# Attention and two MLPs on one core: VectorE's additions moved ahead of its gate ends in MLP 2, early splits taken apart, PSUM accumulators of one bank

## The chip, the cores and the metric

The kernel runs on one core of a Trainium2 chip. The metric is the time of one execution on the device in microseconds (us). All outputs and intermediate results are fp32.

## The reference

The input goes through a chunked attention with memory keys and then through two MLPs. Only MLP 2 is touched by the change:

```
def _moe2_ref(x, w_in, w_out):
    h = x @ w_in                                   # 3072 x 512 @ 512 x 2048
    beta = 1.0
    g = np.where(h >= beta, h, np.where(h <= -beta, 0.0, (h + beta) ** 2 / (4.0 * beta)))
    return (g @ w_out).astype(np.float32)          # 3072 x 2048 @ 2048 x 512

attn_out = _attn_ref(**attn_kwargs)                # softmax(q k) v over 32-token chunks, 8 memory keys
x = attn_out.transpose(0, 2, 1, 3).reshape(B * S, H * D)
x = _moe_ref(x=x, **moe_kwargs)                    # g = h - tanh(h)
return _moe2_ref(x=x, **moe2_kwargs)
```

The gate is the same as max(h, min(relu(h/2 + 1/2)^2, 1)).

## The kernel before

**Arithmetic.** Every fp32 operand of a large matrix product is split into a high part, rounded by ScalarE, and a low part, source minus high part, made by VectorE (`split_to`, L219 to L221). A product of two tiles is then three matmuls: high by high, low by high, high by low. All matmuls of the MLPs have 128 x 128 weights and 512 columns.

**Stages.** Attention and MLP 1 run interleaved over six blocks of 512 tokens (L471 and L506 are MLP 1's two matmuls). From about 574 us on MLP 2 runs, in three blocks (`sb` 0 to 2) of two times 512 tokens. It uses a 2 x 2 scheme of seven block products in place of eight, for both of its matrix products.

**Rounds.** In the first half of a block there are eight rounds `q`. A round has seven products `i` of six matmuls each (`product`), which leave four gates 11, 12, 21 and 22. Three PSUM banks serve a round. Bank a (`qa`, two buffers, from `ps_h`) takes the products 1, 6, 7 and 4, one accumulated on the other; bank b (`qb`) takes 2; bank c (`qc`) takes 5 and 3. Between accumulations ScalarE copies out what was there: u1 after product 1, u2 after 6, v after 5 (L632). The next product on that bank must wait for the copy. The plan's order is: product 1 of round q, then 3 and 4 of round q - 1, then 6, 2, 5 and 7 of round q. In block 0 MLP 1's last 17 output steps stand between.

**Gates.** `gate2` makes a gate in four operations: VectorE adds PSUM and a copy (L642), ScalarE takes relu (L646) and square (L647), and VectorE's *end* takes minimum and maximum (L650). Gate 21 needs no addition and is read from bank a by its relu and by its end. The end is not issued at once: it goes to a list `later`, and `flush` issues the oldest entry behind a later product. Before the change `flush` stood ahead of the gate:

```
name = f"{sb}_{q}"
if i in (3, 6, 2, 7):
    flush()
if i == 1:
    ps[sb, q, "u1"] = take_copy(f"u1_{name}", o)
```

After certain products sums of gates are made (`g_sums`: s1 and s2 at L660 and L661, 21 replaced by a difference at L663).

**Passes.** In the second half of a block seven passes of eight products each go over the rounds' results (`last_product`, L766). Each product takes a split gate or sum (`ghi`, `glo`) as moving operand and adds to two PSUM banks. `prepare` splits; five pairs of slots let it run up to four products ahead, and a table `AHEAD_OF_PASSES` has the first splits made in the late rounds, right behind product 1 (or 5). `done` takes a finished pass out of PSUM. The first passes also carry the sums and splits of the next block's input, on VectorE and ScalarE.

**Order.** The order on each engine is written by hand: an engine works in the order in which the code issues, and waits for what the next instruction needs. SyncE issues all transfers. Temporary 128 x 512 tiles come from a first-in, first-out list of free slots (`take`, `give`); weights stream ten products ahead through the same slots (`load_w`).

Of the kernel before, what the change touches and what calls it, by code (L numbers as in the profile page):

```python
# [8 lines left out]
F32 = mybir.dt.float32  # L9
# [4 lines left out]
AF = mybir.ActivationFunctionType  # L14
ALU = mybir.AluOpType
# [58 lines left out]
def tile_memory_attention_two_mlps(  # L74
# [15 lines left out]
    xsp = ctx.enter_context(tc.tile_pool(name="xsp", bufs=1))  # L90
    dram = ctx.enter_context(tc.tile_pool(name="dram", bufs=1, space=bass.MemoryType.DRAM))
    att = ctx.enter_context(tc.tile_pool(name="att", bufs=2))
    ps_acc = ctx.enter_context(tc.tile_pool(name="ps_acc", bufs=1, space=PSUM))
    ps_h = ctx.enter_context(tc.tile_pool(name="ps_h", bufs=2, space=PSUM))
    pairs = tc.tile_pool(name="ps_a", bufs=1, space=PSUM)
    ps_a = pairs.__enter__()

# [427 lines left out]
        return tag, slot(tag, name, dtype)  # L525

    def give(tag):
        spare.append(tag)

    xc, held, xtags = {}, {}, []  # L530
    XHOME = {1: "xh0", 2: "xl0", 4: "xh1", 3: "xl1", 5: ("k0", "k1"), 6: ("v0", "v1")}
# [136 lines left out]
    bank = {}  # L668

    once = set()  # L670

    def give_second(tag, *key):
        if key in once:
            give(tag)
        once.add(key)

    AHEAD_OF_PASSES = ((6, 1), (6, 5), (7, 1)), ((4, 1), (5, 1), (6, 1), (7, 1))

    def product(e):
        _, sb, q, i = e  # L680
        if i == 1:
            ps[sb, q, "a"] = ps_h.tile([128, 512], F32, tag="h", name=f"qa{sb}_{q}")
        if i == 2:
            ps[sb, q, "b"] = ps_b.tile([128, 512], F32, tag="b", name=f"qb{sb}_{q}")
        if i == 5:
            ps[sb, q, "c"] = ps_b.tile([128, 512], F32, tag="c", name=f"qc{sb}_{q}")
# [12 lines left out]
        if i in (3, 6, 2, 7):  # L699
            flush()  # L700
        if i == 1:
            ps[sb, q, "u1"] = take_copy(f"u1_{name}", o)
        elif i == 6:
            ps[sb, q, "u2"] = take_copy(f"u2_{name}", o)
        elif i == 5:
            ps[sb, q, "v"] = take_copy(f"v_{name}", o)
        elif i == 2:
            gate2(sb, q, "11", o, ps.pop((sb, q, "u1")))
        elif i == 7:
            gate2(sb, q, "22", o, ps.pop((sb, q, "v")))  # L710
        elif i == 3:
            gate2(sb, q, "12", o, ps.pop((sb, q, "u2")))
        else:
            gate2(sb, q, "21", o)
        if 0 < q < HALF - 1 and i == 5:
            g_sums(sb, q - 1, 0)
        if q > 1 and i == 1:
            g_sums(sb, q - 2, 1)
        ahead = AHEAD_OF_PASSES[sb > 0]
        if (q, i) in ahead:  # L720
            prepare(sb, ahead.index((q, i)))
        if sb == 0 and q == 0 and i in (2, 7):
# [5 lines left out]
    def prepare(sb, k):  # L728
        if k >= NG2 or (sb, k) in gsplit:
            return  # L730
        i, q = PASSES[k // HALF], k % HALF
        tag, g = gs[sb, SOURCE[i], q]
        r = prepared[0] % GSETS
        prepared[0] += 1
        hi, lo = slot(f"ghi{r}", f"ghi2_{sb}_{k}", F32R), slot(f"glo{r}", f"glo2_{sb}_{k}", F32R)
        split_to(g, hi, lo)
        if i == 6:
            a12 = gs[sb, "12", q][1]
            nc.vector.tensor_tensor(out=a12, in0=a12, in1=g, op=ALU.subtract)  # L739
# [10 lines left out]
    def last_product(e):  # L750
# [71 lines left out]
    def older(s):  # L822
        output(s)
        fc = steps[s][2]
        if s >= NS - FC:
            give(f"g{fc}")
        if s + 2 < NS:
            split_g(s + 2)
        if s == NS - 1:
            for i in range(W1O):  # L830
                give(f"whi1_{i}")
                give(f"wlo1_{i}")
            for i in range(KC):
# [230 lines left out]
```

## Time and profile before

| | |
|---|---|
| median of 3 runs | 1102.3 us (1102.05 to 1102.45) |
| the profiled execution's own time | 1102.45 us |
| its span in the profile | 1100.7 us |
| TensorE (PE) busy | 1069.3 us, 97%, 7649 matmuls |
| weight loads (PEld) busy | 866.7 us, 79% |
| VectorE (DVE) busy | 792.6 us, 72% |
| ScalarE (ACT) busy | 612.4 us, 56% |
| mean matmul of the passes (L766) | 389 ns, x672 |
| granted TensorE clock | 0.998 over the span |

The profile is one execution on the chip. A row of the timeline has its start in us from the span's start, its length, engine, line of the code, operation, tiles (written<-read), shape and count; in brackets the idle time of the engine before it and who ended it. Matmuls overlap in the pipeline: one is 389 ns long while the next starts some 227 ns after it. The names are those of the code without numbers: `g` a gate, `t` its square, `u` the copies u1 and u2, `ghi` and `glo` the halves of a split.

### The profile page before, as it was taken

How to read it: one execution, taken by the hardware profiler on the slowest of the kernel's cores; microseconds unless marked ns; L12 is line 12 of the kernel's file. 1: busy time of each engine (PE TensorE's matmuls, PEld its weight loads, DVE VectorE, ACT ScalarE, POOL GpSimd, SP SyncE). 2: the span in 40 equal slices, each digit the busy share in tenths (PEclk: the TensorE clock that was granted, in tenths of full speed). 3: DMA queues.
4: the chain of work that ended last, by engine and by line, in shares of the span. 5: the costliest groups of instructions: out<-in, count | busy, mean ns of one | idle time of the engine just before them, and what ended most of it. 6: DMA issues, size and time to landing. Idle time of an engine off the chain costs nothing.

```text
span 1100.7 us, 20755 instructions
## 1 busy us (share of the span) xinstructions
PE 1069.3 (97%) x7649; PEld 866.7 (79%) x7655; DVE 792.6 (72%) x1397; ACT 612.4 (56%) x1085; POOL 42.6 (4%) x38
## 2 busy tenths in 40 slices
PE   7899999999999999999999999999999999998998
PEld 3677888888888888888888788678887778886886
DVE  4799977777777777768866755697466796466854
ACT  3566665544544555444655555656466665566652
POOL 1232221000000000000000000000000000000000
PEclk9999999999999999999999999999999999999999
DMA  9997886897698788649688775677766767765674
GB/s 224 250 263 207 261 245 180 249 296 245 215 298 256 216 262 278 213 150 364 230 282 291 253 245 171 202 244 213 234 191 170 250 212 233 212 191 160 202 203 139
DMA packets 201317, 253.05 MB, mean 230 GB/s; under 512 B 65024, under 2 KB 114176, under 8 KB 201216
## 3 DMA queue, kind: packets, MB, share of 16 engines
q1 hardware_dynamic: 201216, 251.72, 75.3%
q8 instruction: 61, 1.00, 0.4%
q14 instruction: 40, 0.33, 0.1%
HBM read 201.33 MB, written 50.33 MB: 229 GB/s over the span
## 4 chain that ended last, share of the span: by engine, by line
PE 73%; ACT 11%; DVE 10%; SPq 2%; issue 2%; DMA 2%; DVEq 0%; ACTq 0%
PE h L471 24%; PE acc L506 22%; PE acc L766 17%; ACT t L646 5%; ACT t L647 4%; PE qa L693 3%; DVE g L642 3%; DVE g L650 3%; DVE glo L221 2%; PE a L375 1%; PE a L319 1%; PE qc L693 1%; PE b L361 1%; SPq L290 1%; DVE g L739 1%
## 5 line engine op out<-in xcount | busy, mean ns | idle before, releaser
L221 DVE TENSOR_TENSOR glo<-g,ghi 128x512 fp32r<-128x512 f32 x216 | 146.4, 687 | 54.9 <-ACT ghi L220 54.4
L766 PE MATMUL acc<-ghi,inG 128*128 128x512 f32 x672 | 183.2, 389 | 0.0
L481 ACT ACTIVATE g<-h 128x512 f32<-128x512 f32 x96 | 57.4, 598 | 222.7 <-PE h L471 204.5
L220 ACT ACTIVATE ghi<-g 128x512 fp32r<-128x512 f32 x216 | 133.3, 626 | 42.1 <-PE acc L766 23.6
L693 PE MATMUL qa<-xc,inP 128*128 128x512 f32 x576 | 142.4, 393 | 10.8 <-ACT u L632 10.0
L766 PEld LDWEIGHTS acc<-ghi,inG 128*128 128x128 f32 x672 | 126.1, 188 | 26.4
L693 PEld LDWEIGHTS qa<-xc,inP 128*128 128x128 f32 x576 | 106.7, 188 | 38.8 <-ACT u L632 15.6
L482 DVE TENSOR_TENSOR g<-h,g 128x512 f32<-128x512 f32 x96 | 66.2, 690 | 82.3 <-ACT g L481 81.6
L646 ACT ACTIVATE t<-g,half 128x512 f32<-128x512 f32 x72 | 52.2, 724 | 103.8 <-DVE g L642 103.8
L506 PE MATMUL acc<-ghi,whi 128*128 128x512 f32 x384 | 109.2, 398 | 0.0
L766 PE MATMUL acc<-glo,inG 128*128 128x512 f32 x336 | 107.7, 392 | 1.0 <-DVE glo L221 0.5
L506 PE MATMUL acc<-ghi,wlo 128*128 128x512 f32 x384 | 105.8, 390 | 0.0
L506 PE MATMUL acc<-glo,whi 128*128 128x512 f32 x384 | 105.6, 389 | 0.0
L471 PE MATMUL h<-xh,whi 128*128 128x512 f32 (+2 forms) x392 | 105.4, 391 | 0.0
L471 PE MATMUL h<-xl,whi 128*128 128x512 f32 (+2 forms) x392 | 103.8, 386 | 0.1
L471 PE MATMUL h<-xh,wlo 128*128 128x512 f32 (+2 forms) x392 | 103.7, 386 | 0.0
L650 DVE SCALAR_TENSOR_TENSOR g<-t,g 128x512 f32<-128x512 f32 x72 | 49.7, 690 | 51.6 <-ACT t L647 50.0
L471 PEld LDWEIGHTS h<-xl,whi 128*128 128x128 f32 x392 | 73.0, 188 | 15.2 <-DVE xl L406 0.2
L471 PEld LDWEIGHTS h<-xh,wlo 128*128 128x128 f32 x392 | 73.0, 188 | 14.8
L506 PEld LDWEIGHTS acc<-ghi,wlo 128*128 128x128 f32 x384 | 72.1, 188 | 15.6
L506 PEld LDWEIGHTS acc<-glo,whi 128*128 128x128 f32 x384 | 72.1, 188 | 15.1
L471 PEld LDWEIGHTS h<-xh,whi 128*128 128x128 f32 x392 | 71.8, 188 | 15.0 <-ACT xh L401 0.3
(104 smaller groups left out, 1536.7 us busy)
## 6 DMA issues: line engine op xcount, KB each, us to landing
inP<-part SPq DMA_DIRECT2D x168, 256.0 KB, 2.9
inG<-part SPq DMA_DIRECT2D x168, 256.0 KB, 3.0
whi<-w1o SPq DMA_DIRECT2D x80, 256.0 KB, 4.2
wlo<-w1o SPq DMA_DIRECT2D x80, 256.0 KB, 4.6
stage<-w_in SPq DMA_DIRECT2D x32, 512.0 KB, 5.4
stage<-w_out SPq DMA_DIRECT2D x32, 512.0 KB, 4.4
part<-preph SPq DMA_DIRECT2D x64, 256.0 KB, 4.5
part<-prepl SPq DMA_DIRECT2D x48, 256.0 KB, 4.4
```

The lines of the kernel that those rows point to most:

```text
L220: nc.scalar.activation(out=hi, in_=src, func=AF.Copy)
L221: nc.vector.tensor_tensor(out=lo, in0=src, in1=hi.bitcast(F32), op=ALU.subtract)
L471: nc.tensor.matmul(hp, w[:, kc * 128:(kc + 1) * 128], x[:, kc, n0:n1], start=j == 0 and kc == 0, stop=j == 2 and kc == KC - 1,)
L481: nc.scalar.activation(out=g, in_=hp, func=AF.Tanh)
L482: nc.vector.tensor_tensor(out=g, in0=hp, in1=g, op=ALU.subtract)
L506: nc.tensor.matmul(acc_t[dm], w[:, dm * 128:(dm + 1) * 128], g, start=first and j == 0, stop=last and j == 2,)
L642: nc.vector.tensor_tensor(out=g, in0=src, in1=plus[1], op=ALU.add)
L646: nc.scalar.activation(out=t, in_=h, func=AF.Relu, scale=0.5, bias=half)
L647: nc.scalar.activation(out=t, in_=t, func=AF.Square)
L650: nc.vector.scalar_tensor_tensor(out=g, in0=t, scalar=1.0, in1=h, op0=ALU.min, op1=ALU.max)
L693: nc.tensor.matmul(o, w[:, k * 128:(k + 1) * 128], z[k], start=i in (1, 2, 5) and j == 0 and k == 0, stop=j == 2 and k == 1, skip_group_ch ...
L766: nc.tensor.matmul(bank[a][:, c, :], w[:, c * 128:(c + 1) * 128], g, start=first and j == 0, stop=last and j == 2, skip_group_check=True,)
```

## The change

Six edits, all in MLP 2. In a round the gate's addition is issued first and the older end behind it. A split made ahead of the passes issues only the high half at once; the low half goes to a list `rest` that is emptied behind the next product 3, in round 0, or at the next pass product. Block 0 has one such early split fewer. The sums s1 and s2 of round 0 lie in one tile of two halves under a stage tag instead of two slots of the list. Each accumulator of a pass is two tiles of one bank, from pools that are opened when MLP 1 is through. The last block's last output tiles are two single slots.

```diff
     def g_sums(sb, q, part):
...
+            if q == 0:
+                two = wide.tile([128, 2, N], F32, tag="stage3", name=f"s_{sb}_{q}")
+                gs[sb, "s1", q], gs[sb, "s2", q] = (None, two[:, 0, :]), (None, two[:, 1, :])
+            else:
+                gs[sb, "s1", q], gs[sb, "s2", q] = take(f"s1_{sb}_{q}"), take(f"s2_{sb}_{q}")
...
-    AHEAD_OF_PASSES = ((6, 1), (6, 5), (7, 1)), ((4, 1), (5, 1), (6, 1), (7, 1))
+    rest = []
+
+    def rests():
+        while rest:
+            rest.pop(0)()
+
+    AHEAD_OF_PASSES = ((6, 1), (7, 1)), ((4, 1), (5, 1), (6, 1), (7, 1))
...
         name = f"{sb}_{q}"
-        if i in (3, 6, 2, 7):
-            flush()
+        due = later[:1] if i in (3, 6, 2, 7) else []
...
             gate2(sb, q, "21", o)
+        if due:
+            flush()
...
+        if i == 3 or q == 0:
+            rests()
         ahead = AHEAD_OF_PASSES[sb > 0]
         if (q, i) in ahead:
-            prepare(sb, ahead.index((q, i)))
+            prepare(sb, ahead.index((q, i)), ahead=True)
...
+        gsplit[sb, k] = hi, lo
+        if ahead:
+            assert i == 1 and q < HALF - 2
+            nc.scalar.activation(out=hi, in_=g, func=AF.Copy)
+
+            def low():
+                nc.vector.tensor_tensor(out=lo, in0=g, in1=hi.bitcast(F32), op=ALU.subtract)
+                give(tag)
+
+            rest.append(low)
+            return
         split_to(g, hi, lo)
...
-            bank[a] = ps_acc.tile([128, 2, 512], F32, tag=f"acc{1 - a}", name=f"acc{i}_{sb}")
+            bank[a] = [ps_g[0].tile([128, 512], F32, tag=f"g{c}{1 - a}", name=f"acc{i}_{sb}_{c}") for c in range(2)]
+        rests()
         prepare(sb, k)
...
+        y = [y[:, c, :] for c in range(2)]
+        if sb == NSB - 1 and i == 4:
+            y = [take(f"yl{c}")[1] for c in range(2)]
...
         if s == NS - 1:
+            bc.__exit__(None, None, None)
+            sums.__exit__(None, None, None)
+            ps_g.append(ctx.enter_context(tc.tile_pool(name="ps_g", bufs=1, space=PSUM)))
+            ps_g.append(ctx.enter_context(tc.tile_pool(name="ps_d", bufs=1, space=PSUM)))
```

VectorE in block 1, from round 6 to the start of round 7, before and then after. In `g2_1_6_22` the numbers are block, round and gate; a row that reads `t2` is an end, one that reads `qa`, `qb` or `qc` and a copy is an addition, and `glo2_1_3` is the low half of pass product 3.

```order
L650 SCALAR_TENSOR_TENSOR g2_1_6_11_9871<-t2_1_6_11_9873,g2_1_6_11_9871 128x512
L642 TENSOR_TENSOR g2_1_6_22_9900<-qa1_6_9808,v_1_6_9885 128x512
L663 TENSOR_TENSOR g2_1_5_21_9846<-g2_1_5_11_9774,g2_1_5_21_9846 128x512
L221 TENSOR_TENSOR glo2_1_3_9918<-g2_1_3_11_9580,ghi2_1_3_9917 128x512
L650 SCALAR_TENSOR_TENSOR g2_1_6_22_9900<-t2_1_6_22_9902,g2_1_6_22_9900 128x512
L642 TENSOR_TENSOR g2_1_6_12_9930<-qc1_6_9876,u2_1_6_9859 128x512
L650 SCALAR_TENSOR_TENSOR g2_1_6_12_9930<-t2_1_6_12_9932,g2_1_6_12_9930 128x512
L650 SCALAR_TENSOR_TENSOR g2_1_6_21_9943<-t2_1_6_21_9944,qa1_6_9808 128x512
L642 TENSOR_TENSOR g2_1_7_11_9968<-qb1_7_9958,u1_1_7_9914 128x512
```

The same stretch of VectorE after the change:

```order
L644 TENSOR_TENSOR g2_1_6_22_9908<-qa1_6_9817,v_1_6_9894 128x512
L652 SCALAR_TENSOR_TENSOR g2_1_6_11_9879<-t2_1_6_11_9881,g2_1_6_11_9879 128x512
L669 TENSOR_TENSOR g2_1_5_21_9855<-g2_1_5_11_9782,g2_1_5_21_9855 128x512
L644 TENSOR_TENSOR g2_1_6_12_9937<-qc1_6_9885,u2_1_6_9867 128x512
L652 SCALAR_TENSOR_TENSOR g2_1_6_22_9908<-t2_1_6_22_9910,g2_1_6_22_9908 128x512
L758 TENSOR_TENSOR glo2_1_3_9927<-g2_1_3_11_9588,ghi2_1_3_9926 128x512
L652 SCALAR_TENSOR_TENSOR g2_1_6_12_9937<-t2_1_6_12_9939,g2_1_6_12_9937 128x512
L644 TENSOR_TENSOR g2_1_7_11_9976<-qb1_7_9967,u1_1_7_9923 128x512
L652 SCALAR_TENSOR_TENSOR g2_1_6_21_9952<-t2_1_6_21_9953,qa1_6_9817 128x512
```

Each addition moved up past one end, and the low half moved down past the addition and the end of the gates that followed it. ScalarE's order is the same before and after here.

VectorE in block 0, from round 7's last products into the first pass, before and then after:

```order
L642 TENSOR_TENSOR g2_0_7_22_8464<-qa0_7_8376,v_0_7_8453 128x512
L650 SCALAR_TENSOR_TENSOR g2_0_7_22_8464<-t2_0_7_22_8466,g2_0_7_22_8464 128x512
L221 TENSOR_TENSOR glo2_0_3_8480<-g2_0_3_11_7908,ghi2_0_3_8479 128x512
L221 TENSOR_TENSOR glo2_0_4_8484<-g2_0_4_11_8079,ghi2_0_4_8483 128x512
L642 TENSOR_TENSOR g2_0_7_12_8495<-qc0_7_8444,u2_0_7_8427 128x512
L650 SCALAR_TENSOR_TENSOR g2_0_7_12_8495<-t2_0_7_12_8497,g2_0_7_12_8495 128x512
L221 TENSOR_TENSOR glo2_0_5_8522<-g2_0_5_11_8216,ghi2_0_5_8521 128x512
```

The same stretch after the change:

```order
L644 TENSOR_TENSOR g2_0_7_22_8466<-qa0_7_8379,v_0_7_8456 128x512
L652 SCALAR_TENSOR_TENSOR g2_0_7_11_8441<-t2_0_7_11_8443,g2_0_7_11_8441 128x512
L652 SCALAR_TENSOR_TENSOR g2_0_7_22_8466<-t2_0_7_22_8468,g2_0_7_22_8466 128x512
L222 TENSOR_TENSOR glo2_0_2_8484<-g2_0_2_11_7734,ghi2_0_2_8483 128x512
L222 TENSOR_TENSOR glo2_0_3_8488<-g2_0_3_11_7906,ghi2_0_3_8487 128x512
L222 TENSOR_TENSOR glo2_0_4_8492<-g2_0_4_11_8077,ghi2_0_4_8491 128x512
L644 TENSOR_TENSOR g2_0_7_12_8503<-qc0_7_8447,u2_0_7_8429 128x512
L652 SCALAR_TENSOR_TENSOR g2_0_7_12_8503<-t2_0_7_12_8505,g2_0_7_12_8503 128x512
L222 TENSOR_TENSOR glo2_0_5_8530<-g2_0_5_11_8214,ghi2_0_5_8529 128x512
```

Three low halves stand between the end of gate 22 and the addition of gate 12, where two stood. From `glo2_0_5` on VectorE's order through the passes is the same.

ScalarE at the program's end, with what each row waits for, before and then after (`yn4_2` and `yl1` are the second half of the last output):

```order
L220 ACTIVATE ghi2_2_52_12177<-g2_2_4_22_11231 128x512 [waits DVE_49,PE_49]
L220 ACTIVATE ghi2_2_53_12187<-g2_2_5_22_11328 128x512 [waits DVE_49,PE_49]
L220 ACTIVATE ghi2_2_54_12197<-g2_2_6_22_11425 128x512 [waits DVE_49,PE_49]
L220 ACTIVATE ghi2_2_55_12207<-g2_2_7_22_11518 128x512 [waits DVE_49,PE_49]
L803 ACTIVATE yn4_2_12235<-acc1_2_11523 128x512 [waits DMAHW2_49,DMAHW3_49,DMAHW1_49,DVE_49]
```

The same place after the change:

```order
L221 ACTIVATE ghi2_2_52_12191<-g2_2_4_22_11241 128x512 [waits DVE_49,PE_49]
L221 ACTIVATE ghi2_2_53_12201<-g2_2_5_22_11338 128x512 [waits DVE_49,PE_49]
L221 ACTIVATE ghi2_2_54_12211<-g2_2_6_22_11435 128x512 [waits DVE_49,PE_49]
L221 ACTIVATE ghi2_2_55_12221<-g2_2_7_22_11528 128x512 [waits DVE_49,PE_49]
L833 ACTIVATE yl1_12251<-acc1_2_1_11535 128x512 [waits PE_49]
```

The last copy waited for VectorE and for transfers; now it waits for TensorE alone.

## Rows read from the trace of the kernel before

**Rows 1.** Busy times by stretch: bounds, length, PE, PEld, DVE, ACT, POOL, PEclk, DMA, GB/s.

```profile
616.00:698.50 82.50, 79.27 (x344) 63.94 (x344) 50.32 (x83) 48.59 (x83) 0.00 (x0) 1.00 0.67 206
698.50:740.00 41.50, 40.73 (x177) 32.58 (x177) 36.66 (x61) 26.64 (x47) 0.00 (x0) 1.00 0.75 242
708.50:734.50 26.00, 25.36 (x110) 19.98 (x108) 25.93 (x44) 15.01 (x26) 0.00 (x0) 1.00 0.77 259
740.00:815.00 75.00, 75.00 (x332) 62.10 (x331) 47.13 (x74) 44.52 (x75) 0.00 (x0) 1.00 0.74 214
815.00:858.00 43.00, 39.18 (x168) 30.61 (x167) 26.16 (x41) 27.99 (x47) 0.00 (x0) 1.00 0.64 176
858.00:898.00 40.00, 39.72 (x173) 31.82 (x173) 35.37 (x59) 25.37 (x44) 0.00 (x0) 1.00 0.76 248
974.00:1016.60 42.60, 38.84 (x167) 30.27 (x166) 25.86 (x41) 27.91 (x46) 0.00 (x0) 1.00 0.60 176
```

**Rows 2.** TensorE's waits from 574 us: total, times, longest, in us.

```profile
PE qa L693 <- ACT u L632: 10.0, 12, 1.2
```

**Rows 3.** Timeline of TensorE in block 1's late rounds.

```profile
834.16 3.01 PE L693 MATMUL qa<-xc,inP 128*128 128x512 f32 x12 [1.21 <-ACT u L632]
837.01 1.54 PE L693 MATMUL qc<-xc,inP 128*128 128x512 f32 x6
...
845.25 3.06 PE L693 MATMUL qa<-xc,inP 128*128 128x512 f32 x12 [1.22 <-ACT u L632]
...
856.34 1.65 PE L693 MATMUL qa<-xc,inP 128*128 128x512 f32 x6 [1.19 <-ACT u L632]
```

**Rows 4.** Timeline of VectorE and ScalarE in one of these rounds.

```profile
828.41 0.62 ACT L220 ACTIVATE ghi<-g 128x512 fp32r<-128x512 f32 x1
829.07 0.69 DVE L221 TENSOR_TENSOR glo<-g,ghi 128x512 fp32r<-128x512 f32 x1 [1.86 <-ACT ghi L220]
829.68 0.68 DVE L650 SCALAR_TENSOR_TENSOR g<-t,g 128x512 f32<-128x512 f32 x1
830.28 0.68 DVE L642 TENSOR_TENSOR g<-qc,u 128x512 f32<-128x512 f32 x1
831.00 0.72 ACT L646 ACTIVATE t<-g,half 128x512 f32<-128x512 f32 x1 [1.96 <-DVE g L642]
...
832.42 0.69 DVE L650 SCALAR_TENSOR_TENSOR g<-t,g 128x512 f32<-128x512 f32 x1 [1.46 <-ACT t L647]
...
833.53 0.58 ACT L632 ACTIVATE u<-qa 128x512 f32<-128x512 f32 x1
```

**Rows 5.** Timeline before block 0's first stall.

```profile
614.62 0.69 DVE L650 SCALAR_TENSOR_TENSOR g<-t,g 128x512 f32<-128x512 f32 x1
...
615.22 0.69 DVE L642 TENSOR_TENSOR g<-qc,u 128x512 f32<-128x512 f32 x1
...
620.70 0.58 ACT L632 ACTIVATE u<-qa 128x512 f32<-128x512 f32 x1
...
621.33 0.50 PE L693 MATMUL qa<-xc,inP 128*128 128x512 f32 x1 [0.81 <-ACT u L632]
```

**Rows 6.** Timelines of TensorE and VectorE in block 0's first passes.

```profile
697.06 1.65 PE L693 MATMUL qa<-xc,inP 128*128 128x512 f32 x6 [1.20 <-ACT u L632]
...
710.29 1.29 DVE L221 TENSOR_TENSOR glo<-g,ghi 128x512 fp32r<-128x512 f32 x2
...
711.03 0.72 PE L766 MATMUL acc<-glo,inG 128*128 128x512 f32 x2 [0.46 <-DMA a<-yd]
...
734.63 0.50 PE L766 MATMUL acc<-glo,inG 128*128 128x512 f32 x1 [0.27 <-DVE glo L221]
```

**Rows 7.** Timeline of the last two copies out of PSUM.

```profile
1095.85 0.69 DVE L805 COPY yn<-acc 128x512 f32<-128x512 f32 x1 [5.89 <-PE acc L766]
...
1096.57 0.60 ACT L803 ACTIVATE yn<-acc 128x512 f32<-128x512 f32 x1 [7.35 <-DVE yn L805]
```

**Rows 8.** Transfers by issue: count, KB each, median us to landing.

```profile
part<-preph SPq DMA_DIRECT2D x64, 256.0 KB, 4.5
```

More of the change, by code (lines that the diff above doesn't have):

```diff
@@ L92, in tile_memory_attention_two_mlps @@
     att = ctx.enter_context(tc.tile_pool(name="att", bufs=2))
-    ps_acc = ctx.enter_context(tc.tile_pool(name="ps_acc", bufs=1, space=PSUM))
     ps_h = ctx.enter_context(tc.tile_pool(name="ps_h", bufs=2, space=PSUM))
+    sums = tc.tile_pool(name="ps_acc", bufs=1, space=PSUM)
+    ps_acc = sums.__enter__()
     pairs = tc.tile_pool(name="ps_a", bufs=1, space=PSUM)
@@ L527, in give @@
     def give(tag):
-        spare.append(tag)
+        if tag is not None:
+            spare.append(tag)
     xc, held, xtags = {}, {}, []
@@ L657, in g_sums @@
         if part == 0:
-            gs[sb, "s1", q], gs[sb, "s2", q] = take(f"s1_{sb}_{q}"), take(f"s2_{sb}_{q}")
+            if q == 0:
[3 more added lines that the diff above has]
+                gs[sb, "s1", q], gs[sb, "s2", q] = take(f"s1_{sb}_{q}"), take(f"s2_{sb}_{q}")
             s1, s2 = gs[sb, "s1", q][1], gs[sb, "s2", q][1]
@@ L670, in tile_memory_attention_two_mlps @@
     once = set()
+    ps_g = []
     def give_second(tag, *key):
@@ L683, in product @@
         if i == 2:
-            ps[sb, q, "b"] = ps_b.tile([128, 512], F32, tag="b", name=f"qb{sb}_{q}")
+            ps[sb, q, "b"] = (ps_g[1] if ps_g else ps_b).tile([128, 512], F32, tag="b", name=f"qb{sb}_{q}")
         if i == 5:
-            ps[sb, q, "c"] = ps_b.tile([128, 512], F32, tag="c", name=f"qc{sb}_{q}")
+            ps[sb, q, "c"] = (ps_g[1] if ps_g else ps_b).tile([128, 512], F32, tag="c", name=f"qc{sb}_{q}")
         o = ps[sb, q, {2: "b", 5: "c", 3: "c"}.get(i, "a")]
@@ L726, in tile_memory_attention_two_mlps, with prepare @@
     SOURCE = {1: "11", 2: "12", 6: "s2", 5: "s1", 7: "21", 3: "12", 4: "22"}
-    def prepare(sb, k):
+    def prepare(sb, k, ahead=False):
         if k >= NG2 or (sb, k) in gsplit:
@@ L743, in prepare @@
             give(tag)
-        gsplit[sb, k] = hi, lo
     prepared = [0]
@@ L766, in last_product @@
             nc.tensor.matmul(
-                bank[a][:, c, :], w[:, c * 128:(c + 1) * 128], g,
+                bank[a][c], w[:, c * 128:(c + 1) * 128], g,
                 start=first and j == 0, stop=last and j == 2, skip_group_check=True,
@@ L791, in done @@
         if i in (1, 6, 5):
-            kept[i] = [take_copy(f"k{name}_{c}", a[:, c, :]) for c in range(2)]
+            kept[i] = [take_copy(f"k{name}_{c}", a[c]) for c in range(2)]
             return
@@ L799, in done @@
                 tag, t = kept[plus][c]
-                nc.vector.tensor_tensor(out=y[:, c, :], in0=a[:, c, :], in1=t, op=ALU.add)
+                nc.vector.tensor_tensor(out=y[c], in0=a[c], in1=t, op=ALU.add)
                 give(tag)
             elif c:
-                nc.scalar.activation(out=y[:, c, :], in_=a[:, c, :], func=AF.Copy)
+                nc.scalar.activation(out=y[c], in_=a[c], func=AF.Copy)
             else:
-                nc.vector.tensor_copy(out=y[:, c, :], in_=a[:, c, :])
+                nc.vector.tensor_copy(out=y[c], in_=a[c])
             b = 2 * sb + block
-            nc.sync.dma_start(out=out[(dm + c) * 128:(dm + c + 1) * 128, b * N:(b + 1) * N], in_=y[:, c, :])
+            nc.sync.dma_start(out=out[(dm + c) * 128:(dm + c + 1) * 128, b * N:(b + 1) * N], in_=y[c])
     late = [[] for _ in range(4 * HALF)]
@@ L999, in tile_memory_attention_two_mlps @@
     pairs.__exit__(None, None, None)
-    ps_b = ctx.enter_context(tc.tile_pool(name="ps_b", bufs=1, space=PSUM))
+    bc = tc.tile_pool(name="ps_b", bufs=1, space=PSUM)
+    ps_b = bc.__enter__()
     events = 0
```

## The prediction

> **What bounds the kernel now.** I read the busy times by stretch first, then TensorE's waits, then the timeline of the stretches where they lie.
>
> Up to 616 us and again from 740 to 815 us TensorE has no idle time: 332 matmuls in 75.00 us [rows 1], so a product of six takes 1.36 us and a round of seven products 9.5. There no edit elsewhere can gain anything. TensorE loses time in two kinds of stretch. The late rounds of products: 82.50 - 79.27 = 3.23 us idle in block 0, 43.00 - 39.18 = 3.82 in block 1, 42.60 - 38.84 = 3.76 in block 2; and the first passes: 0.77 in block 0, 0.28 in block 1 [rows 1]. Nearly all of it, 10.0 us in twelve waits, is a product that waits for ScalarE's copy u [rows 2]. A stall costs more than its idle time. A matmul's row reaches about 0.16 past the next one's start (0.39 long, as the profile's table has it, and 75.00/332, some 0.227 apart), which the idle time leaves out, and the six matmuls behind a stall take 1.65 where an undisturbed product takes 1.54 [rows 3], another 0.11. So each stall costs its idle time plus 0.27: five stalls in block 0's rounds 3.23 + 1.35 = 4.58, four in block 1's 3.82 + 1.08 = 4.90, four in block 2's 3.76 + 1.08 = 4.84, three in block 0's passes 0.77 + 0.81 = 1.58, three in block 1's 0.28 + 0.81 = 1.09. That is all there is to win on TensorE: 17.0 us.
>
> Neither VectorE nor ScalarE lacks time in those rounds: 26.16 and 27.99 us busy of 43.00 [rows 1]. What is too long is a chain. In rounds 4 to 7 of blocks 1 and 2 the round takes 11.09 us (834.16 to 845.25, and to 856.34 [rows 3]) instead of 9.5. Inside it [rows 4]: ScalarE rounds g to ghi at 828.41; VectorE, in order, waits 1.86 for that, does glo (829.07), the end of gate 22 (829.68), and only then the addition of gate 12 (830.28), whose product had been done for over a microsecond; ScalarE idles 1.96 until its relu at 831.00, works through four gate steps, and copies u at 833.53. The product that needs u starts at 834.16.
>
> **The change part by part.** *Additions ahead of ends, low halves taken apart* (one answer, since one chain holds both). I lay a round out from the start of its product 1, at 1.36 a product, with a result readable 1.54 after a product's start (length of a product's row [rows 3]), 0.60 from one VectorE operation to the next, 0.72 from an addition to its relu, 1.42 from a relu to the earliest end behind its square [rows 4].
> - Product 3 starts at 1.36 and is readable at 2.90. The addition of gate 12 now stands in front: 2.90, relu 3.62, square, end not before 5.04. The end of 22 and glo go into the gap, 3.5 and 4.1. ghi, asked for at product 1, follows ScalarE's copy at about 2.8 and is done by 3.4, before the relu wants the engine. So the split costs ScalarE and VectorE 0.6 each and the chain nothing.
> - relu and square of gate 21 follow at about 4.9 and 5.7, u (product 6 readable at 5.62) at 6.2, done 6.8. Product 7 needs it at 8.16: 1.4 spare, where today it is 1.2 late.
> - Addition of 11 at 6.98, then the end of 21, s1, s2 at 7.6, 8.2 and 8.8, done at 9.5. Product 7 is readable at 9.70: addition of 22 then, relu 10.4, square 11.2, the next u1 at 11.7 to 12.3. The next product 6 needs it at 9.5 + 4.08 = 13.6: 1.3 spare.
>
> So all four stalls of block 1's rounds go (4.90) and of block 2's (4.84). What is late next is nothing on TensorE. In block 0 the four stalls from 684 on are the same chain and go. The fifth, at 621.33, comes from u at 620.70 behind an addition at 615.22 that stood behind an end (614.62) [rows 5]. It needs u 0.98 earlier (0.81 + 0.16). This swap gives 0.60, and the same swap at the three gates before it on that chain 0.60 each. I take 2.4, and the stall goes: 4.58 in all. If only the one swap counted, 0.4 + 0.1 of it would stay.
>
> *One split fewer ahead of block 0's passes.* VectorE is saturated from 708.5 to 734.5, 25.93 busy of 26.00 with 44 operations [rows 1], so there every operation counts. glo of pass product 6 starts today at 710.29, 13.2 after product 7 of round 7 (697.06), and TensorE waits for it until 711.03 (the bracket names a transfer, but the row is the matmul that reads this glo, and glo was done 0.06 before), then twice more, last at 734.63 [rows 6]. New order, from that product 7: addition of 22 at 1.5, relu 2.3, end of 22 at 3.7, now three glo (4.3 to 6.1), addition of 12 at 6.1, relu 6.8, its end at 8.2; gate 21's two steps to about 9.4, ghi to 10.0, then glo, end, s1, s2 and the glo in question at 12.5. That is 0.7 earlier although one glo was added. Through the saturated stretch the 0.7 is kept, so of 1.58 lost about 0.9 stays, gain 0.6 (with an end at 0, and at 1.58 if the stretch had slack that I can't see). In block 1 one glo stands there instead of three: the same steps give 11.3, 1.9 before 13.2; the loss there is 1.09 and goes.
>
> *Single-bank accumulators, single output tiles.* At the end ScalarE copies the second half at 1096.57, behind VectorE's copy of the first half at 1095.85, which began when the last matmul was done [rows 7]; two engines read one two-bank tile, and the second waits for the first. With a tile per bank ScalarE waits for TensorE alone and starts at 1095.85: 0.72 earlier, and the output transfer behind it too, which ends the span. The same wait inside the passes sits where ScalarE has room, so I cost it at 0.
>
> *The sum s in a stage tile, other slots by the shifted list.* No instruction is added, so 0. Some ScalarE instructions of block 0's rounds 4 to 6 now wait for other transfers than before, since they get a slot that was stored from. A store lands after 4.5 us [rows 8]; those slots come several rounds later. Bounds 0 and one landing, 4.5; I take 0. A rule speaks against the first part: the Trainium skill ("PSUM — Partial Sum Buffer", Engine vs sequencer instructions) states that "ScalarE/VectorE/GpSimdE queues are strict FIFO". The trace agrees (glo's 1.86 holds the ready addition behind it, rows 4); by that rule an early addition holds ready ends just as well, which is the first rival.
>
> **Sum.** 4.58 + 4.90 + 4.84 + 0.6 + 1.09 + 0.72 = 16.7 us. The profiled execution took 1102.45 us (span 1100.7 and 1.75 around it): 1085.7. The median is 0.15 below that execution, so **1085.6 us**.
>
> **Rivals.** *A new wait in place of the old.* The addition at the head of the queue waits for its product, and ends, sums and glo behind it come late. For: only 0.2 us lie between s2's end (9.5) and the addition of 22 (9.70). Against: behind it u1 still has 1.3 spare. If half of the rounds' 14.3 us came back, 1085.6 + 7.2 = 1092.8.
>
> *The passes take it back.* Where VectorE is saturated, order gains nothing and the extra glo costs 0.60 + 0.27. Then the passes' 1.7 gain is gone and 0.9 is added: 1088.2. For: the 25.93 of 26.00; against: VectorE waits for ScalarE before 708.5, so a shorter chain does start that stretch sooner. Beside it the Trainium skill ("VectorE: DVE Perf Modes", Rules for kernel authors) says to minimise the count of operations; by that rule the rounds too would gain nothing, yet there VectorE is busy only 26.16 of 43.00.
>
> *It doesn't do what it says.* The u copies were late for another reason, and only the tail is won: 1101.6. Rows 4 speak against it, link by link.
>
> *Slower: the bank comes back late.* The end of gate 21 reads the bank that product 1 of two rounds on writes. It now stands behind an addition, at 7.6 to 8.3 of a round; product 1 needs it at 9.5. If it came 2 us later than that, product 1 would wait 0.8 + 0.27 in all 24 rounds, 26 us against 16.7 won: 1111. It decides from about 1.6 us late (0.4 + 0.27, times 24). Nothing in the rows delays it so.
>
> **Chances.** Forecast 0.80 (alone 1084 to 1087.5), new wait 0.08, passes 0.06, no effect 0.03, slower 0.03. Within 0.2% is 2.2 us, about what a measurement of this kernel can't tell from no change. Faster holds the first three, 0.94; same 0.03; slower 0.03. The range reaches from 1083.8 (the passes' loss all gone too, and a little more) to 1090 (the passes' rival, or one landing of 4.5).
>
> **What would show it.** TensorE's waits for u near zero, against 10.0; rounds of 9.5 us to the last in every block; VectorE's additions starting with their product's end, the ends behind; one or two short waits for glo left in block 0's first passes, none in block 1's; ScalarE's last copy beside VectorE's. Wrong would be: a product 1 that waits for VectorE's end, ScalarE waiting for a transfer in block 0's rounds, or rounds over 9.7.

## The result and the profile after

The changed kernel takes 1085.54 us (median of 5 runs, 1084.08 to 1086.91) against 1102.45 (5 runs, 1102.05 to 1103.27): ratio 0.9845, 95% interval 0.9831 to 0.9859. The forecast was 1085.6, range 1083.8 to 1090. Its profiled execution took 1086.91 us with a span of 1085.1.

Start again with the busy times by stretch; columns as in [rows 1]. The first row holds block 0's first passes, the other two the late rounds of blocks 1 and 2.

```profile
690.00:733.00 43.00, 42.60 (x186) 34.33 (x185) 36.56 (x61) 27.52 (x47) 0.00 (x0) 1.00 0.76 243
800.00:858.00 58.00, 58.00 (x257) 48.05 (x256) 40.65 (x63) 43.18 (x72) 0.00 (x0) 1.00 0.67 194
975.00:1040.00 65.00, 65.00 (x289) 53.81 (x288) 49.00 (x78) 43.15 (x72) 0.00 (x0) 1.00 0.68 202
```

The late rounds have no idle time left; block 0's passes keep 0.40 us. TensorE's waits from 560 us on (total, times, longest) are down from the twelve of [rows 2] to this one line:

```profile
PE acc L793 <- DVE glo L222: 0.3, 1, 0.3
```

Next the timeline of VectorE, ScalarE and TensorE in a late round of block 1 (start, length, engine, line; in brackets the idle time before). It answers to [rows 3, 4]. The round's product 1 starts at 830.85: it is the last six of the eight matmuls in the first row, the first two of which belong to the product before.

```profile
830.40 1.98 PE L706 MATMUL qa<-xc,inP 128*128 128x512 f32 x8
...
832.21 1.52 PE L706 MATMUL qc<-xc,inP 128*128 128x512 f32 x6
...
833.62 0.62 ACT L755 ACTIVATE ghi<-g 128x512 fp32r<-128x512 f32 x1
833.77 0.69 DVE L644 TENSOR_TENSOR g<-qc,u 128x512 f32<-128x512 f32 x1 [0.76 <-PE qc L706]
834.38 0.68 DVE L652 SCALAR_TENSOR_TENSOR g<-t,g 128x512 f32<-128x512 f32 x1
834.50 0.73 ACT L648 ACTIVATE t<-g,half 128x512 f32<-128x512 f32 x1 [0.26 <-DVE g L644]
834.98 0.68 DVE L758 TENSOR_TENSOR glo<-g,ghi 128x512 fp32r<-128x512 f32 x1
...
837.04 0.58 ACT L634 ACTIVATE u<-qa 128x512 f32<-128x512 f32 x1
...
837.85 0.69 DVE L644 TENSOR_TENSOR g<-qb,u 128x512 f32<-128x512 f32 x1 [1.24 <-PE qb L706]
838.46 0.68 DVE L652 SCALAR_TENSOR_TENSOR g<-t,qa 128x512 f32<-128x512 f32 x1
...
839.01 1.98 PE L706 MATMUL qa<-xc,inP 128*128 128x512 f32 x8
839.17 0.69 DVE L666 TENSOR_TENSOR s<-g,g 128x512 f32<-128x512 f32 x1
...
839.90 0.69 DVE L667 TENSOR_TENSOR s<-s,g 128x512 f32<-128x512 f32 x1
...
840.64 0.69 DVE L644 TENSOR_TENSOR g<-qa,v 128x512 f32<-128x512 f32 x1
```

Read VectorE's column: the addition of gate 12 starts 0.04 after its product's row ends (832.21 + 1.52), the end of gate 22 and glo fill the time behind it, and ScalarE's relu waits 0.26 instead of 1.96. u is done at 837.62; the product that needs it starts at 839.01, unhindered, 1.39 later. In [rows 3] it stood still for 1.21.

What is left is in block 0's first passes, in answer to [rows 6]: three short waits for glo, at 708.29, 727.68 and 731.90. By the spacing of matmuls they take 0.21, 0.21 and 0.46; the view of waits above has the third alone, the others leave too small a gap for it. The first and the third: at 707.55 VectorE begins two glo, the first is done at 708.24, and TensorE goes on at 708.29.

```profile
707.55 1.29 DVE L222 TENSOR_TENSOR glo<-g,ghi 128x512 fp32r<-128x512 f32 x2
...
708.29 0.50 PE L793 MATMUL acc<-glo,inG 128*128 128x512 f32 x1
...
731.90 0.50 PE L793 MATMUL acc<-glo,inG 128*128 128x512 f32 x1 [0.29 <-DVE glo L222]
```

And the end of the program, in answer to [rows 7]:

```profile
1080.67 0.69 DVE L835 COPY yl<-acc 128x512 f32<-128x512 f32 x1 [5.22 <-PE acc L793]
1080.93 0.39 PE L793 MATMUL acc<-glo,inG 128*128 128x512 f32 x1
1081.35 0.60 ACT L833 ACTIVATE yl<-acc 128x512 f32<-128x512 f32 x1 [6.62 <-PE acc L793]
```

ScalarE's copy now waits for TensorE alone. From the last matmul's start to its end it is 1.02 us, where it was 1.75 (the last matmul began at 1095.42).

**A yardstick for small differences.** MLP 2's first matmul starts at 574.1 us in the profile before and at 576.6 in this one, though the work up to there is the same; over the thirteen profiles of this study it lies between 573.8 and 577.5. In this one the loss is a pause of TensorE near 40 us, with a lower granted clock behind it (the third number from the end of a row):

```profile
40.00:42.00 2.00, 1.20 (x4) 1.11 (x5) 0.14 (x1) 0.00 (x0) 1.29 (x1) 0.68 0.46 104
42.00:44.00 2.00, 2.00 (x9) 2.00 (x8) 0.36 (x1) 0.60 (x1) 0.00 (x0) 0.50 0.51 150
```

So effects of 1 us are read below from the length of MLP 2, first matmul's start to last matmul's start, which doesn't contain this: 521.31 before, 504.31 after, 504.40 when the changed kernel was profiled again. Its 2220 matmuls at the undisturbed spacing of 0.22667 take 503.0; so before lost 18.3 us there, after 1.3.

### The profile page after: what moved, and what is told of

The parts are those of the page before. It is cut to its first block, busy times and chain, and to the rows that moved or that the text cites. A ratio compares the mean times of both kernels' runs of the same rounds, so it can differ in the third digit from the quotient of the medians.

```text
span 1085.1 us, 20769 instructions
## 1 busy us (share of the span) xinstructions
PE 1065.2 (98%) x7655; PEld 870.1 (80%) x7655; DVE 794.2 (73%) x1397; ACT 614.7 (57%) x1085; POOL 42.5 (4%) x38
## 4 chain that ended last, share of the span: by engine, by line
PE 97%; ACT 1%; DVE 1%; issue 0%; ACTq 0%; DVEq 0%
PE h L472 25%; PE acc L507 24%; PE acc L793 21%; PE qa L706 12%; PE qc L706 6%; PE qb L706 3%; PE a L376 1%; PE a L320 1%; PE start_tx L941 1%; PE b L362 1%; PE b L396 1%; ACT e L350 0%; PE start_a L320 0%; PE start_a L376 0%; PE start_tx L396 0%
## 5 line engine op out<-in xcount | busy, mean ns | idle before, releaser
L222 DVE TENSOR_TENSOR glo<-g,ghi 128x512 fp32r<-128x512 f32 x206 | 140.2, 687 | 35.8 <-ACT ghi L221 34.9
L221 ACT ACTIVATE ghi<-g 128x512 fp32r<-128x512 f32 x206 | 127.4, 626 | 46.5 <-PE acc L793 23.7
L706 PE MATMUL qa<-xc,inP 128*128 128x512 f32 x576 | 140.1, 389 | 0.0
L507 PE MATMUL acc<-ghi,whi 128*128 128x512 f32 x384 | 109.2, 399 | 0.0
L507 PE MATMUL acc<-ghi,wlo 128*128 128x512 f32 x384 | 105.7, 390 | 0.0
L507 PE MATMUL acc<-glo,whi 128*128 128x512 f32 x384 | 105.7, 389 | 0.0
L507 PEld LDWEIGHTS acc<-ghi,wlo 128*128 128x128 f32 x384 | 72.1, 188 | 15.4
L507 PEld LDWEIGHTS acc<-glo,whi 128*128 128x128 f32 x384 | 72.1, 188 | 15.2
L175 DVE TENSOR_TENSOR wlo<-raw,whi 128x512 fp32r<-128x512 f32 x112 | 79.6, 710 | 4.7 <-ACT whi L168 4.7
```

The source lines that it names most:

```text
L175: nc.vector.tensor_tensor(out=lo, in0=r, in1=hi.bitcast(F32), op=ALU.subtract)
L221: nc.scalar.activation(out=hi, in_=src, func=AF.Copy)
L222: nc.vector.tensor_tensor(out=lo, in0=src, in1=hi.bitcast(F32), op=ALU.subtract)
L507: nc.tensor.matmul(acc_t[dm], w[:, dm * 128:(dm + 1) * 128], g, start=first and j == 0, stop=last and j == 2,)
L706: nc.tensor.matmul(o, w[:, k * 128:(k + 1) * 128], z[k], start=i in (1, 2, 5) and j == 0 and k == 0, stop=j == 2 and k == 1, skip_group_ch ...
```

## Experiments

| kernel | median us (runs) | ratio to before, 95% | MLP 2, us | lost there |
|---|---|---|---|---|
| before | 1102.45 (5) | | 521.31 | 18.3 |
| changed | 1085.54 (5) | 0.9845 (0.9831 to 0.9859) | 504.31 | 1.3 |
| e1 early splits whole | 1085.19 (4) | 0.9826 (0.9811 to 0.9841) | 504.32 | 1.3 |
| e2 ends first | 1087.67 (4) | 0.9861 (0.9835 to 0.9887) | 505.47 | 2.5 |
| e3 two-bank accumulators | 1086.24 (1) | | 504.37 | 1.4 |
| e4 third split, round 5 | 1090.98 (5) | 0.9874 (0.9856 to 0.9891) | 508.72 | 5.7 |
| e5 the same, other buffer | 1084.55 (4) | 0.9825 (0.9812 to 0.9839) | 503.76 | 0.8 |
| e6 four splits | 1084.81 (5) | 0.9831 (0.9818 to 0.9844) | 503.14 | 0.2 |
| e7 changed, again | 1086.60 (4) | 0.9843 (0.9830 to 0.9857) | 504.40 | 1.4 |
| e8 output tile | 1086.17 (1) | | 504.32 | 1.3 |
| e9 two more copies | 1087.11 (1) | | 504.93 | 2.0 |
| e10 four more copies | 1105.48 (1) | | 525.89 | 22.9 |
| e11 two more, splits whole | 1095.19 (1) | | 514.82 | 11.8 |

Each ratio goes by the runs of before on the same chip (1103.80 and 1103.82 for e1 to e8).

### Which of the two edits does it: e1 and e2

e1 issues an early split whole again:

```diff
-            prepare(sb, ahead.index((q, i)), ahead=True)
+            prepare(sb, ahead.index((q, i)))
```

> The changed kernel with one part undone: the early splits are issued whole again (ghi, then glo at once, ahead of gate 12's addition). The theory (one loop through VectorE and ScalarE): in the kernel before, the 11.09 us of a late round are a loop glo - end 22 - addition 12 - relu, square, relu, square - end 21 - addition 11 - relu, square - end 11 - addition 22 - relu, square, u1, ghi - glo, without TensorE in it. With the additions ahead three ends (22, 21, 11) leave it, at least 3 x 0.60: 11.09 - 1.8 = 9.3, below TensorE's 9.52. So the rounds stay free of stalls although glo is back in the chain, u is done some 0.3 us before it is needed, and the time is 1085.5 to 1087. Rival (the two edits share the gain about evenly): half of the rounds' 14.3 us comes back, 1092.5, with TensorE waiting about 0.6 a late round for u.

Measured: as the loop says. MLP 2 takes 504.32 us, TensorE waits for no u. A late round of block 1 in this kernel's timeline:

```profile
821.55 0.62 ACT L221 ACTIVATE ghi<-g 128x512 fp32r<-128x512 f32 x1
822.20 0.69 DVE L222 TENSOR_TENSOR glo<-g,ghi 128x512 fp32r<-128x512 f32 x1 [1.26 <-ACT ghi L221]
822.81 0.69 DVE L644 TENSOR_TENSOR g<-qc,u 128x512 f32<-128x512 f32 x1
...
826.07 0.58 ACT L634 ACTIVATE u<-qa 128x512 f32<-128x512 f32 x1
...
826.94 0.39 PE L706 MATMUL qa<-xc,inP 128*128 128x512 f32 x1
```

VectorE still stands 1.26 for ghi with the ready addition behind it, as in [rows 4], and it costs nothing: u is done at 826.65, 0.29 before it is needed.

e2 issues the ends first again:

```diff
-        due = later[:1] if i in (3, 6, 2, 7) else []
+        if i in (3, 6, 2, 7):
+            flush()
...
-        if due:
-            flush()
```

> The changed kernel with the other part undone: each gate end is issued ahead of the next addition again, the low halves stay apart. The theory (one loop): without glo the loop goes from square 22 straight to end 22; by the rows of the kernel before that takes 1.57 us out of 11.09, leaving 9.52, just TensorE's 9.52. So in blocks 1 and 2 stalls of 0 to 0.2 us a round; in block 0, whose rounds carry more VectorE work, up to 0.5 in some; in its passes the low halves come about 0.6 later. 1086 to 1090. Rival (even shares): 1092.5, waits for u of about 0.6 in each late round. Rival (the low half was nothing, the order of additions and ends was all): stalls of over 1 us a late round, 1100.

Measured: no stall in the rounds of blocks 1 and 2, one in block 0, and nothing more in its passes. Timeline of e2 before that stall:

```profile
617.18 0.69 DVE L652 SCALAR_TENSOR_TENSOR g<-t,g 128x512 f32<-128x512 f32 x1
...
617.78 0.69 DVE L644 TENSOR_TENSOR g<-qc,u 128x512 f32<-128x512 f32 x1
...
623.27 0.58 ACT L634 ACTIVATE u<-qa 128x512 f32<-128x512 f32 x1
...
623.91 0.50 PE L706 MATMUL qa<-xc,inP 128*128 128x512 f32 x1 [0.83 <-ACT u L634]
```

It is the stall of [rows 5] again, 0.83 against 0.81, so that one belongs to the additions; block 0's early splits come in rounds 6 and 7, so no low half could matter for it. The other twelve round stalls vanish with either edit. In block 0 this is not a clean case, since e1 and e2 both also lack the early split at (6, 5) (e6 below has it back beside both edits, and no stall); the eight stalls of blocks 1 and 2 are one. Shares can't be given: the loop was 1.57 us a round longer than TensorE's 9.52, and by its rows each edit alone takes out at least that much.

No kernel undoes both edits and keeps the other four, so e1 and e2 leave open whether those four did it. Two traces answer that. In the kernel before, block 1's rounds 4 to 7 have an early split and a stall each, the rounds before them neither. Here are u and the product that needs it in round 2:

```profile
801.78 0.58 ACT L632 ACTIVATE u<-qa 128x512 f32<-128x512 f32 x1
...
803.67 0.39 PE L693 MATMUL qa<-xc,inP 128*128 128x512 f32 x1
```

And in e2, in a late round of block 1, with an early split whose low half is out of the way:

```profile
828.81 0.58 ACT L634 ACTIVATE u<-qa 128x512 f32<-128x512 f32 x1
...
830.68 0.39 PE L706 MATMUL qa<-xc,inP 128*128 128x512 f32 x1
```

u is done 1.31 before it is needed in the first and 1.29 in the second. So in blocks 1 and 2 the stalls of the kernel before came with the early split, and the other four edits move u by nothing that shows. Against the 1.39 of the changed kernel and the 0.29 of e1 this also gives each edit's worth in spare time beside the other: 1.1 us a round for the low half, 0.1 for the additions.

### What the second edit then buys: e9, e10, e11

If both edits do the same, the second must show as spare time. These kernels put n more copies on ScalarE ahead of u (e9: n = 2; e10: n = 4; e11: e1 with n = 2). The copies' result is overwritten by the gate's end.

```diff
         nc.scalar.activation(out=t, in_=t, func=AF.Square)
+        if i == "21" and q < HALF - 1:
+            for _ in range(n):
+                nc.scalar.activation(out=g, in_=src, func=AF.Copy)
```

> The changed kernel with two more ScalarE copies (of the product's bank, into a tile that the gate's end overwrites) behind the square of gate 21, and so ahead of u, in rounds 1 to 7 of each block; about 0.5 us each by the rows of u and v. The theory (u has 1.39 us to spare in a round: in the changed kernel it is done at 837.62 and the product that needs it starts at 839.01): u comes 1.0 later, still in time, no wait for u; MLP 2 stays at 504.3 us, within 0.5. Rival (the spare is not there to use, since ends and sums move too): waits for u of 0.2 us or more in the late rounds.

> The same with four more copies. The theory: u comes 1.9 to 2.1 later, 0.5 to 0.75 too late, and about 0.1 more is lost behind each wait; in 7 rounds of blocks 1 and 2 and the last two of block 0, 16 waits, MLP 2 about 11 us longer (8 to 14): 515 us. Rival (TensorE's rounds have more slack than the layout says): under 3 us longer.

> The kernel with the early splits whole (the first experiment) and the two more copies. The theory (there u has only 0.29 us to spare in the rounds with an early split: done at 826.65, needed at 826.94): u comes 0.7 too late in rounds 4 to 7 of blocks 1 and 2 and in rounds 6 and 7 of block 0, ten waits of about 0.7 and 0.1 behind each, MLP 2 about 8 us longer (6 to 10): 512 us, while the changed kernel with the same two copies stays at 504.3. Rival (taking the splits apart buys nothing, as the first experiment alone would suggest): no more than 1 us apart from the changed kernel with the two copies.

e9 has no wait for u in the late rounds; MLP 2 is 0.6 longer, a little over the expected 0.5, of which 0.35 is one short stall at 622.9 in block 0. TensorE's waits in e10 and in e11:

```profile
PE qa L709 <- ACT u L634: 16.2, 18, 1.6
```

```profile
PE qa L709 <- ACT u L634: 7.1, 10, 0.7
```

e11 has exactly the ten waits expected, in rounds 4 to 7 of blocks 1 and 2 and 6 and 7 of block 0, each 0.84 to 0.88 of TensorE's time. MLP 2 is 10.5 us longer, a little over the expected 6 to 10: each wait was dearer than the expected 0.7, and a short stall at 621.1 in block 0 (0.3) was not counted. e10 has 18 instead of 16 (two more in block 0), and they are dearer: 1.03 in the late rounds, 21.6 us in all, where 8 to 14 was expected. The size was off, since these copies follow each other 0.62 apart and were costed at about 0.5; whether that comes from the one tile that they write or the one bank that they read wasn't tried. Timeline of e10:

```profile
834.59 2.47 ACT L652 ACTIVATE g<-qa 128x512 f32<-128x512 f32 x4
...
836.95 0.59 ACT L634 ACTIVATE u<-qa 128x512 f32<-128x512 f32 x1
...
837.60 0.73 PE L709 MATMUL qa<-xc,inP 128*128 128x512 f32 x2 [0.87 <-ACT u L634]
```

u starts 2.36 behind the first copy: 2.36 - 1.39 = 0.97 late, and 1.03 was lost. With two copies u comes 1.11 later (838.44 - 837.33 in e9): within 1.39, and 0.82 over the 0.29 of e1. So the spare times read from the two timelines are real: beside the early additions, taking the splits apart is worth nothing in this kernel's time, and 1.1 us a round of room. The 1.29 of e2 is a reading; no run put copies into e2.

### The tail: e3 and e8

e3 makes each pair of accumulators one two-bank tile again; e8 keeps them apart and writes both last outputs into one stage tile.

```diff
-            bank[a] = [ps_g[0].tile([128, 512], F32, tag=f"g{c}{1 - a}", name=f"acc{i}_{sb}_{c}") for c in range(2)]
+            two = ps_g[0].tile([128, 2, 512], F32, tag=f"acc{1 - a}", name=f"acc{i}_{sb}")
+            bank[a] = [two[:, c, :] for c in range(2)]
```

```diff
         if sb == NSB - 1 and i == 4:
-            y = [take(f"yl{c}")[1] for c in range(2)]
+            pass
```

> The changed kernel with two-bank accumulator tiles again in MLP 2's passes, the last outputs still in single tiles. The theory (readers wait for each other by the tile): VectorE's last copy starts only when the very last matmul is done, and ScalarE's copy starts behind VectorE's, 0.7 us after that matmul's end instead of 0.03; the tail is 0.7 us longer, nothing else changes by more than 0.2. Rival (the shared output tile made the wait): ScalarE's last copy still starts with the last matmul's end.

> The changed kernel with the last two outputs in one two-half stage tile again, the accumulators in single banks. The theory (the accumulator tile alone made ScalarE's last copy wait): VectorE's copy still starts with the first half's last matmul, ScalarE's with the second half's, from the last matmul's start to ScalarE's end 1.0 us as in the changed kernel. Rival (two engines writing one tile wait as well): ScalarE starts behind VectorE's copy, up to 0.3 later, 1.3 us.

The last two copies of e3, then of e8:

```profile
1080.00 0.69 DVE L836 COPY yl<-acc 128x512 f32<-128x512 f32 x1 [5.89 <-PE acc L794]
...
1080.72 0.60 ACT L834 ACTIVATE yl<-acc 128x512 f32<-128x512 f32 x1 [7.35 <-DVE yl L836]
```

```profile
1080.12 0.69 DVE L835 COPY yn<-acc 128x512 f32<-128x512 f32 x1 [5.21 <-PE acc L793]
...
1080.79 0.60 ACT L833 ACTIVATE yn<-acc 128x512 f32<-128x512 f32 x1 [6.62 <-PE acc L793]
```

In e3 ScalarE waits for VectorE as in [rows 7], and the stretch from the last matmul's start to its end is 1.75 us; in e8 it waits for TensorE, 1.02. The accumulator tile made the whole wait; the single output tiles do nothing. Elsewhere the two-bank tile costs nothing that shows: MLP 2 takes 504.37, against 504.31.

### The last 1.3 us: e4, e5, e6

e4 adds a third early split in block 0.

```diff
-    AHEAD_OF_PASSES = ((6, 1), (7, 1)), ((4, 1), (5, 1), (6, 1), (7, 1))
+    AHEAD_OF_PASSES = ((5, 1), (6, 1), (7, 1)), ((4, 1), (5, 1), (6, 1), (7, 1))
```

> The changed kernel with a third early split in block 0: (5, 1) beside (6, 1) and (7, 1). The theory (the 1.2 us that are left in block 0's first passes are VectorE running without a gap, each operation there counts): one glo (0.60) and one ghi (0.62) leave that stretch; the three waits for glo (0.21, 0.21 and 0.46 of TensorE's time, 0.11 more behind each) fall to at most 0.2 in all; the rounds keep their 1.4 us of spare for u and show no stall. About 1.0 to 1.2 us less than the changed kernel: 1084.4. Rival (the wait is ScalarE's chain behind round 7, and order decides): no change, 1085.5. Rival (round 5 can't take another split): a stall for u of 0.2 to 1 us comes back in round 5 or 6 of block 0, 1085.5 to 1086.5.

Both rivals and the theory missed: MLP 2 takes 508.72, 4.4 us longer than in the changed kernel (the medians, 1090.98 against 1085.54, are from different series). The passes did most of what was expected: two of the three waits are gone, but the third keeps 0.43, where 0.2 in all was expected. And round 5 of block 0 had a new stall. Its timeline:

```profile
674.96 0.39 PE L507 MATMUL acc<-ghi,wlo 128*128 128x512 f32 x1
...
675.19 0.39 PE L507 MATMUL acc<-glo,whi 128*128 128x512 f32 x1
675.39 0.63 ACT L755 ACTIVATE ghi<-g 128x512 fp32r<-128x512 f32 x1 [10.05 <-PE acc L507]
675.92 0.71 ACT L648 ACTIVATE t<-g,half 128x512 f32<-128x512 f32 x1
...
678.72 2.15 PE L706 MATMUL qc<-xc,inP 128*128 128x512 f32 x6 [3.14 <-issue]
```

ScalarE stood for 10.05 us at one ghi. Its buffer, the first of five pairs, was being read by the last step of MLP 1 (L507): the last matmul that takes its ghi is the first row, which ends at 675.35, and the new ghi starts at 675.39. The relu of gate 12 stood behind it; that gate's addition had run at 668.82. This is the strict FIFO of the Trainium skill ("PSUM — Partial Sum Buffer", Engine vs sequencer instructions); the trace agrees, with a far larger price than the 1.86 of [rows 4]. Then TensorE's clock fell. Busy times of e4 (the granted clock is the third number from the end of a row):

```profile
676.00:679.00 3.00, 0.28 (x1) 0.30 (x2) 2.37 (x4) 2.94 (x7) 0.00 (x0) 1.00 0.00 0
679.00:680.00 1.00, 1.00 (x5) 0.78 (x4) 1.00 (x3) 0.97 (x3) 0.00 (x0) 0.80 0.00 0
680.00:683.00 3.00, 3.00 (x9) 2.32 (x8) 1.74 (x3) 1.75 (x4) 0.00 (x0) 0.50 0.45 162
683.00:690.00 7.00, 7.00 (x32) 5.77 (x32) 4.48 (x7) 5.41 (x9) 0.00 (x0) 1.00 0.94 267
```

TensorE went on at 678.72, behind the 3.1 us pause, with matmuls 0.23 to 0.31 apart. From 680 to 683 the granted clock is 0.50 (1.2 GHz), and they start 0.43 apart. To test that the buffer is the cause, e5 keeps e4's split and begins with the next pair, which MLP 1 has left by then:

```diff
-    prepared = [0]
+    prepared = [1]
```

> The kernel of the run before this one (third early split in block 0, at product 1 of round 5), but MLP 2's splits begin with the second of the five pairs of ghi and glo instead of the first. The theory (the 10.1 us that ScalarE stood at that ghi were the wait for its buffer, which the last step of MLP 1 reads until 675.2; the pair after it is read for the last time four steps earlier): ScalarE doesn't wait there, TensorE has no stall in the rounds and no half clock behind one, and of block 0's three waits for glo two are gone (one of 0.43 + 0.11 was left there). MLP 2 loses about 0.7 us instead of the 5.7 of the run before and the 1.3 of the changed kernel: 1084.7. Rival (round 5 has no room for a split): a stall of 1 us or more stays in round 5, 1086 or more.

Measured: no wait, no pause, no fall of the clock; MLP 2 takes 503.76, 0.8 lost (expected 0.7). Round 5 has room for a split; the buffer had none. e6 has four early splits, two of them behind MLP 1's last step:

```diff
-    AHEAD_OF_PASSES = ((6, 1), (7, 1)), ((4, 1), (5, 1), (6, 1), (7, 1))
+    AHEAD_OF_PASSES = ((5, 5), (6, 1), (6, 5), (7, 1)), ((4, 1), (5, 1), (6, 1), (7, 1))
```

> The changed kernel with four early splits in block 0, two of them behind the last step of MLP 1: (5, 5), (6, 1), (6, 5) and (7, 1). The theory (each glo taken out of block 0's first passes brings the rest 0.60 earlier; the three waits there are 0.21 to 0.46 long; u has 1.4 us to spare in a round, more than the 0.6 of another ghi): none of the three waits is left, none comes up in the rounds, MLP 2 loses under 0.2 us against the changed kernel's 1.34, 1.2 us less: 1084.3. Rival (the waits hang on the chain behind round 7): 0.5 or more stays. Rival (two splits are too much for rounds 6 and 7): waits for u or v of 0.2 us and more in rounds 6 and 7.

> The changed kernel itself, as the yardstick beside the others: 1085.5, MLP 2 from its first matmul to its last in 504.3 us; where its first matmul starts (576.6 in the profile so far, 574.0 to 577.5 in other kernels that share the code up to there) differs from execution to execution.

The view of waits shows none of TensorE's in MLP 2, which takes 503.14 us, 0.2 above the undisturbed spacing. The first passes of e6:

```profile
704.00:730.00 26.00, 26.00 (x116) 21.40 (x114) 25.93 (x44) 15.24 (x26) 0.00 (x0) 1.00 0.83 278
```

VectorE is as saturated there as before (25.93 of 26.00 with 44 operations, [rows 1]), but it comes early enough. e6's 1084.81 us (1084.38 to 1086.68) lies below the changed kernel's 1086.60 on the same chip (1084.94 to 1087.62), but the ranges overlap, and the changed kernel's first five runs had a median of 1085.54; the 1.2 us are shown by the length of MLP 2, not by the time.

## Why the prediction was right, step by step

Gains by step, the measured ones from the spacing of matmuls in the two profiles of before and after:

| step | predicted | measured |
|---|---|---|
| block 0's rounds | 4.58 | 4.75 |
| block 1's rounds | 4.90 | 5.21 |
| block 2's rounds | 4.84 | 5.21 |
| block 0's passes | 0.6 | 0.48 |
| block 1's passes | 1.09 | 1.11 |
| block 2's passes | not counted | 0.24 |
| tail | 0.72 | 0.73 |
| sum | 16.7 | 17.7 |
| before MLP 2 | 0 | -2.5 |
| last transfers | 0 | 0.4 |
| span | 16.7 | 15.6 |

- **Rounds.** The mechanism held link by link. The layout put addition 12, u and addition 22 at 2.90, 6.2 and 9.70 of a round; counted from 830.85 the profile has them at 2.92, 6.19 and 9.79. The spare of u, predicted 1.4, is 1.39. A stall was priced too low, at idle time plus 0.27: the losses come to about 0.06 more each, for matmuls behind it that start 0.24 apart.
- **The number.** That the median came within 0.1 us of the forecast is luck. The sum was 1.0 too small, the two executions differ by 2.5 ahead of MLP 2 and by 0.4 behind it, and the five runs of the changed kernel spread over 2.8. What the runs bear out is the list of steps.
- **One answer for both edits.** It hid that either suffices for the eight round stalls of blocks 1 and 2 (e1, e2). The sum stood. glo's 1.86 need not go for the stalls to go (e1 keeps a wait of 1.26 there), but by spare time it was the larger part: 1.1 of room a round against 0.1.
- **Block 0's stall at 621.** Costed by a sum of swaps, 2.4 against 0.98 needed. Counted from MLP 2's first matmul, u starts at 46.6 in the kernel before (620.70 - 574.11) and at 43.8 after (620.38 - 576.62), 2.8 earlier. e2 has the stall and e1 has not, so the additions cure it.
- **Block 0's passes.** The glo in question was put 12.5 behind product 7 of round 7 and stands at 12.6 (707.55 - 694.93); the addition of 12 at 6.18, where 6.1 was expected. From that product to the matmul behind the third wait it is 0.60 less than before (731.90 - 694.93 against 734.63 - 697.06), as forecast; 0.11 of that is the slow matmuls behind the stall at 697.06, which the table counts with the rounds, and 0.48 is the passes' own. The 0.9 said to stay was 1.3, since the loss before was 1.76 and not 1.58, and three short waits are left where one or two were named.
- **Tail.** Right in size and cause; e3 and e8 show that the edit is the accumulators', not the output tiles'.
- **Slots at nothing.** No TensorE wait and none of ScalarE's larger waits from 560 us on is for a transfer. Undoing the stage tile by itself wasn't tried.
- **Rivals.** The new wait: addition 22 does now start behind s2 (840.64), 0.1 after its product's row ends, and nothing follows from it. The bank: no product 1 waits. Wrong in the other direction was the 0 for the part before MLP 2: unchanged code, but 2.5 us off between these two executions, which is more than all errors of the sum.

## What to carry to other kernels

Where two engines hand work back and forth, add up the whole loop and compare it with the round of the engine that should bound it: here the stalls were gone once it was shorter by any amount, and what more an edit did was room that only later work could spend. Read the room (from the end of the last hand-over to the start of what needs it) in each kernel with one edit undone: equal times can hide unequal edits. Before an operation is moved ahead in an in-order queue, look up who reads its output buffer last, not only whether its inputs are ready. When executions differ by more than the edit is worth, compare the length of the stage that was edited.

## What the runs showed of the hardware

- In e4 a pause of 3.1 us on TensorE was followed, about 1 us after it went on, by a fall of the granted clock to 0.50 (1.2 GHz) from 680 to 683, with matmuls 0.43 apart. It cost about 1.7 us on top of the pause: block 0's rounds lose 5.0, of which 3.3 is the pause.
- On VectorE an operation that reads the result of the one before it starts 0.73 behind it (s2 behind s1, 839.17 to 839.90), an independent one 0.60 to 0.61 (837.85 to 838.46).
- Copies from a PSUM bank on ScalarE started 0.62 apart when they read the same bank and wrote the same tile (four in 2.47), where u and the ghi behind it start 0.47 apart (833.15 to 833.62).
